# Two output rows assembled from a split last weight, in a recurrence followed by a soft mixture of experts on one Trainium2 core

## The chip, the core and the metric

The kernel runs on one core of a Trainium2 chip. The core has a matrix engine (TensorE, PE in the profile; its weight loads are PEld), a vector engine (VectorE, DVE), a scalar engine (ScalarE, ACT), a general engine (GpSimd, POOL) and a sync engine (SyncE, SP), which here issues the loads of the inputs and all stores. Weights are loaded from GpSimd's queue, which converts them to bf16 on the way. All transfers share 16 transfer engines. TensorE writes to PSUM, eight banks of 2 KB in each of 128 partitions, and the results are taken from there by VectorE or ScalarE.

The metric is the device time of one execution in microseconds, lower being better.

## The reference

Inputs are x and f_logit (4 batches, 5056 steps, 256 channels), a lower bound per channel, phi (256 x 32), w1 (8 experts, 256 x 1024) and w2 (8 experts, 1024 x 256). The output has 20224 rows of 256 channels, float32.

```python
def _attn_ref(x, f_logit, lower_bound):
    sig = 1.0 / (1.0 + np.exp(-f_logit))
    f = lower_bound + (1.0 - lower_bound) * sig
    i = 1.0 - f
    for t in range(S):
        h = f[:, t] * h + i[:, t] * x[:, t]
        y[:, t] = h

def _moe_ref(x, phi, w1, w2):
    logits = x @ phi                                # x: the rows of y, 20224 x 256
    d = softmax of logits over the rows             # one column per slot, 32 slots
    slot_input = d.T @ x                            # 8 experts x 4 slots, 256 channels
    for e in range(E):
        slot_out[e] = np.maximum(slot_input[e] @ w1[e], 0.0) @ w2[e]
    c = softmax of logits over the 32 slots
    return c @ slot_out
```

The two lines with "softmax of" stand for the written-out maximum, exponential and division. The slot inputs need every row of all batches, and every output row needs the slot outputs: no output can be finished before the last input has been read and the last weight applied.

## The kernel before, in words

**The first part** walks over units n of up to 512 steps of one batch: ten groups of four batches, 40 units. For each unit it loads f_logit and x, forms the sigmoid on ScalarE (L234), multiplies it with x on GpSimd (L245), turns both to channels by TensorE transposes (L249, L264), scans on VectorE (L332), turns the result back (L345, copied out at L364), and takes logits (L378) and their exponentials. The exponentials of all rows stay in `etall`, bf16, with 32 partitions for each batch: partition 32 b + s is slot s of batch b. Rows of 128 such columns are turned to tokens (L399) and multiplied with the scan's result into `slot_ps` (L428), which becomes the slot inputs. The order of all this is written by hand (`manual_schedule`, L157); the loop is at L499 to L595. Weights are loaded at units named in `W_AT`, by `load_w` on GpSimd's queue; the last weight, w2 of expert 7, comes in three pieces, of 4, 2 and 2 of its 8 chunks of 128 hidden channels (L144). In some units `idle` (L177) issues matmuls whose result isn't used, into the second half of the PSUM tile `slot_bank`, whose first half is `slot_ps`.

**The turn from the first part to the output** is at L596 to L710. `row_sums` (L407) sums the exponentials of the 32 slots for each row into `sums`, which lies in the PSUM tile `tail`; their reciprocals go to `rrow` and are the scales of the output rows. The slot inputs are taken from `slot_ps`, summed over the batches and turned to channels by four matmuls into `sin_ps` (L616 to L620), which is a part of `tail` too. They are scaled into `sin` (L631 on VectorE, L632 on ScalarE). The first layer (L648) makes `hi`, twice [128, 1024]: 32 partitions for each of four experts. The hidden values are turned by TensorE (L663) into `hid` (experts 0 to 3) and `wide` (experts 4 to 7, written out for all four batches). The second layer goes into one PSUM tile, `so_ps` (L696): 8 chunks of experts 4 to 7, and between them the sum over experts 0 to 3. `spin` (L707) then issues eight matmuls whose result isn't used. VectorE scales `so_ps` by `rcs`, the reciprocal of the sum of each slot's exponentials, into `slot_out` (L708), which has 32 partitions for each batch, and GpSimd makes from it `slot_bd` (L710), in which two batches stand side by side for one matmul.

**The output part** (from L713) has three kinds of stage, all made of one or several matmuls of `etall` with `slot_out` or `slot_bd`, an eviction with a scale by VectorE (`by_vector`, L717) or ScalarE (`by_scalar`, L721), and stores from SyncE's queue. `pieces` does the first 2048 rows of one batch, 16 rows for each partition, in five stores of growing size: 2, 2, 2, 4 and 6 rows for each partition. `by_rows` does the last block, two batches at a time (L760). `rest` does the last 64 rows of each batch. `whole` does the first 2048 rows of the other batches, one store each, and `couple` (L801) the second 2048 rows of two batches. The buffers come from pools: `osb` in SBUF, which takes the place of the first part's weights and loads, `pfirst` in PSUM, eight banks, and later `pout`. A pool that takes the place of released ones waits, at its first use, for the last use of everything in them.

Of the kernel before, what the change touches and what calls it, by code (L numbers as in the profile page):

```python
# [18 lines left out]
def kernel(  # L19
# [61 lines left out]

    nc.vector.tensor_copy(ident, ident_f)

    def rep_constants(b):
# [77 lines left out]
    with tc.tile_pool(name="sp2", bufs=3) as sp2, \  # L162
# [336 lines left out]
        for n in range(n_unit):  # L499
# [15 lines left out]
            else:  # L515
# [38 lines left out]
                if n in (n_unit - 5, n_unit - 4):  # L554
                    idle(2)
                elif n == SINGLE - 2:
                    idle(1, True)
                elif 2 * B <= n < n_unit - 4 and n % (2 * B) in (1, 5, 6, 7):
                    idle(1)
# [55 lines left out]
        nc.vector.tensor_copy(slot_sb, slot_ps)  # L615
        sin_ps = tail[:, 0, ds(G // 2, DC * NS)].rearrange("p (o s) -> p o s", o=DC)  # L616
        slot_v = slot_sb.rearrange("p (c o) -> p o c", o=DC)
# [6 lines left out]
    with tc.tile_pool(name="ew", bufs=1) as ew, \  # L624
# [16 lines left out]
        for q in range(E // Q):  # L641
            hi = ew.tile([P, F], BF16, name=f"hi{q}")
            for k in range(2):
# [10 lines left out]
                else:  # L654
                    nc.vector.tensor_scalar_max(hi[:, ds(k * H, H)], hi_ps, 0.0)
            his.append(hi)
        cs_ps = pm.tile([P, 1], F32, name="cs_ps", tag="pm")
        rcs = ew.tile([P, 1], F32, name="rcs")
        for q in range(E // Q):
# [4 lines left out]
            if q == 0:  # L664
                nc.tensor.matmul(cs_ps, rep2, cs1, start=True, stop=True)
                src = ht_ps.rearrange("p f (j s) -> p f j s", s=NS)[:, :, :, ds(0, SPE)]
                src = bass.AP(tensor=src.tensor, offset=src.offset,
                              ap=[list(src.ap[0]), [P, FC], [NS + SPE, Q], [1, SPE]])
                dst = hid[:, :, :, ds(0, SPE)]
                dst = bass.AP(tensor=dst.tensor, offset=dst.offset,  # L670
                              ap=[list(dst.ap[0]), [Q * NS, FC], [NS + SPE, Q], [1, SPE]])
                nc.scalar.copy(dst, src)
                nc.vector.reciprocal(rcs, cs_ps)
                continue
            for j in range(Q):
# [17 lines left out]
        nc.vector.reciprocal(rrow[:, :wide_r], rs_ps[:, :wide_r])  # L693
        for j in range(Q):
            for fc in range(FC):
                nc.tensor.matmul(so_ps, wide[:, fc, j].rearrange("p b s -> p (b s)"),  # L696
                                 w2_sb[Q + j][:, fc], start=j == 0 and fc == 0,
                                 stop=j == Q - 1 and fc == FC - 1, skip_group_check=True)
            if j == 0:
                nc.tensor.matmul(so_ps, rep2, so4, start=False, stop=False,  # L700
                                 skip_group_check=True)
                row_sums(2)
            if j == 1:
                q = n_grp * R - 1
                nc.vector.reciprocal(rrow[:, wide_r:q], rs_ps[:, wide_r:q])
                nc.vector.reciprocal(rrow[:, q, ds(0, B // 2)], rs_ps[:, q, ds(0, B // 2)])
        spin(tail[:, 1], 8, P)  # L707
        nc.vector.tensor_scalar_mul(slot_out, so_ps, rcs)  # L708
# [4 lines left out]
    held.close()  # L713
    with tc.tile_pool(name="osb", bufs=3) as osb:

# [21 lines left out]
        def pieces(i, b):  # L737
            dst = rows_of(i, b)
            ob = osb.tile([P, blocks[i][1], D], F32, name="ob", tag="ob")
            r0 = 0  # L740
            for k in (1, 1, 1, 2, 3):
                for j in range(2):
# [29 lines left out]
        end = len(blocks) - 1  # L772
        with tc.tile_pool(name="pfirst", bufs=8, space=PSUM) as pfirst:
            pieces(0, 0)
            by_rows(end, 0)
            by_rows(end, 1)
# [57 lines left out]
        rest()  # L834
        for b in range(1, B):
            whole(0, b)
# [33 lines left out]
```

## Time and profile before

| what | value |
|---|---|
| three runs | 196.96, 197.34, 197.62 us; median 197.34 |
| the profiled execution | 197.01 us |
| its span, first to last instruction | 195.2 us |
| mean granted TensorE clock | 0.845 of full speed |
| PE, PEld busy | 150.6 us (77%), 108.7 us (56%) |
| DVE, ACT, POOL busy | 142.0 us (73%), 138.8 us (71%), 103.1 us (53%) |
| HBM read and written | 58.23 MB, 20.71 MB |

A row of the timeline has the start in microseconds from the span's start, the time from the first start to the last end of the merged instructions, the engine, the line, and out<-in with shapes and count; in brackets stands the idle time before it and what ended it. A row of windows has the stretch, its length, the busy time of PE, PEld, DVE, ACT and POOL with the number of instructions, then the granted clock, the busy share of the 16 transfer engines and GB/s. For loads that convert float32 to bf16 the GB/s count the bytes written. A row of the chain of waits has start, length and what it was. In the lines of slices each digit is a tenth of the share, for one of 40 equal slices of the span. Matmuls overlap: their spacing, not the length of one, is the rate.

### The profile page before, as it was taken

Reading aid. Unit: us, or ns where it says so; the run is one execution under the profiler, and the core shown is the slowest. Engines: PE = TensorE matmul, PEld = TensorE weight load, DVE = VectorE, ACT = ScalarE, POOL = GpSimd, SP = SyncE. Lnnn points to the kernel's source line nnn. Section 1 sums busy time; section 2 is a strip of 40 time slices with the busy share of each in tenths; the row PEclk is TensorE's granted clock in tenths of the full one; section 3 lists DMA queues with packets and bytes.
Section 4 is the critical chain, followed back from the end, with each engine's and each line's share of the span. In section 5 each row is a group of like instructions: output and inputs, shape, how many; then the busy total and the mean of one; then the engine's idle time right before and its main releaser. Section 6 shows DMA issues by size and latency. Waiting matters only on the chain.

```text
span 195.2 us, 3283 instructions
## 1 busy us (share of the span) xinstructions
PE 150.6 (77%) x1222; PEld 108.7 (56%) x1222; DVE 142.0 (73%) x175; ACT 138.8 (71%) x192; POOL 103.1 (53%) x78
## 2 busy tenths in 40 slices
PE   0684896898998979989798976999997999980000
PEld 0474775765786657857576755766872663420000
DVE  2666699799699999999999999824288867770000
ACT  3686778599988998989988698724068788991000
POOL 2584888756798949776888979592030000000000
PEclk9998799699699999999999999999985555555555
DMA  6999999999999999999999999999949999999995
GB/s 203 415 433 428 426 425 421 430 426 411 326 428 426 423 334 405 423 425 414 324 418 418 235 212 214 214 212 211 170 165 428 425 431 426 430 433 430 430 430 218
DMA packets 12145, 70.75 MB, mean 362 GB/s; under 512 B 1361, under 2 KB 1874, under 8 KB 7650
## 3 DMA queue, kind: packets, MB, share of 16 engines
q1 hardware_dynamic: 9504, 62.13, 76.3%
q0 software_dynamic: 2624, 8.42, 21.8%
q8 instruction: 9, 0.15, 0.3%
q14 instruction: 6, 0.05, 0.1%
q10 hardware_dynamic: 2, 0.00, 0.0%
HBM read 58.23 MB, written 20.71 MB: 404 GB/s over the span
## 4 chain that ended last, share of the span: by engine, by line
PE 36%; DVE 28%; DMA 17%; ACT 4%; issue 4%; SPq 1%; POOL 0%; ACTq 0%
DVE h L332 17%; DMA w_t<-in_moe_w_dram 7%; PE op L801 7%; PE sp L249 7%; PE op L727 6%; DMA w_sb<-in_moe_w_dram 6%; PE hp L345 5%; DVE ht L364 5%; PE up L264 4%; DMA f_t<-in_f_logit_dram 4%; DVE h L319 3%; DVE oc L717 2%; PE op L760 2%; ACT s_t L234 1%; PE lg L378 1%
## 5 line engine op out<-in xcount | busy, mean ns | idle before, releaser
L245 POOL TENSOR_TENSOR u_t<-s_t,x_t 128x1024 bf16<-128x1024 bf16 (+1 forms) x39 | 82.4, 2129 | 24.5 <-ACT s_t L234 14.2
L332 DVE TENSOR_TENSOR_SCAN h<-a,h,up 128x512 bf16<-128x512 f32 x64 | 78.1, 1267 | 9.0 <-PE up L264 4.3
L234 ACT ACTIVATE s_t<-f_t 128x2048 bf16<-128x2048 f32 (+2 forms) x22 | 38.1, 1736 | 2.9 <-DMA f_t<-in_f_logit_dram 2.9
L345 PE MATMUL hp<-ident_f,h 128*128 128x128 f32 (+1 forms) x160 | 29.3, 307 | 8.4 <-DVE ht L364 6.3
L297 ACT ACTIVATE a<-sp,lbs 128x1024 f32<-128x1024 bf16 x28 | 29.6, 1112 | 4.6 <-PE sp L249 4.5
L345 PEld LDWEIGHTS hp<-ident_f,h 128*128 128x128 f32 (+1 forms) x160 | 23.2, 206 | 17.0 <-DVE ht L364 11.5
L249 PE MATMUL sp<-ident_f,s_t 128*128 128x128 f32 x144 | 23.7, 315 | 7.0 <-ACT s_t L234 5.7
L249 PEld LDWEIGHTS sp<-ident_f,s_t 128*128 128x128 f32 x144 | 19.6, 164 | 8.7 <-ACT s_t L234 6.5
L264 PE MATMUL up<-ident_f,u_t 64*128 64x64 f32 x224 | 21.4, 236 | 2.4 <-POOL u_t L245 2.4
L264 PEld LDWEIGHTS up<-ident_f,u_t 64*128 64x128 f32 x224 | 17.0, 144 | 7.1 <-POOL u_t L245 2.8
L721 ACT ACTIVATE ob<-op,rrow 128x256 f32<-128x256 f32 x32 | 12.4, 478 | 9.1 <-PE op L727 8.7
L364 ACT COPY ht<-hp 128x512 f32<-128x512 f32 (+1 forms) x21 | 12.2, 583 | 7.9 <-PE hp L345 7.9
L304 ACT ACTIVATE a<-sp,lbs 128x512 f32<-128x512 bf16 (+2 forms) x16 | 13.2, 868 | 2.9 <-PE sp L249 2.7
L183 PE MATMUL slot_ps<-rep,ident_f 128*128 128x256 f32 x42 | 14.2, 426 | 0.0
L364 DVE COPY ht<-hp 128x512 f32<-128x512 f32 (+1 forms) x19 | 12.7, 668 | 1.0 <-PE hp L345 1.0
L801 PE MATMUL op<-slot_bd,etall 64*128 64x512 bf16 x32 | 13.1, 627 | 0.0
L812 ACT ACTIVATE oc<-op,rrow 128x256 f32<-128x256 f32 x32 | 12.2, 486 | 0.8 <-PE op L801 0.3
L727 PE MATMUL op<-slot_out,etall 32*128 32x256 bf16 x64 | 12.6, 375 | 0.1
L806 DVE TENSOR_TENSOR oc<-op,rrow 128x1024 f32<-128x1024 f32 x8 | 9.7, 1223 | 3.4 <-PE op L801 3.4
L717 DVE TENSOR_TENSOR ob<-op,rrow 128x1024 f32<-128x1024 f32 (+2 forms) x12 | 9.8, 862 | 2.2 <-DMA out_dram<-ob 1.1
L727 PEld LDWEIGHTS <-etall 32*128 32x128 bf16 x64 | 8.9, 153 | 3.8 <-issue 1.3
L378 PE MATMUL lg<-h,phi 128*32 128x512 bf16 (+1 forms) x80 | 9.9, 389 | 0.2 <-ACT et L402 0.2
(109 smaller groups left out, 168.9 us busy)
## 6 DMA issues: line engine op xcount, KB each, us to landing
f_t<-in_f_logit_dram SPq DMA_DIRECT2D x14, 1024.0 KB, 11.2
x_t<-in_x_dram SPq DMA_DIRECT2D x14, 1024.0 KB, 9.5
out_dram<-oc SPq DMA_DIRECT2D x4, 2048.0 KB, 13.1
w_sb<-in_moe_w_dram POOLq DMA_DIRECT2D x14, 512.0 KB, 9.5
out_dram<-ob SPq DMA_DIRECT2D x3, 2048.0 KB, 9.6
f_t<-in_f_logit_dram SPq DMA_DIRECT2D x8, 512.0 KB, 7.0
x_t<-in_x_dram SPq DMA_DIRECT2D x8, 512.0 KB, 6.1
out_dram<-oc SPq DMA_DIRECT2D x4, 896.0 KB, 6.0
```

What stands on the lines that cost most here:

```text
L183: nc.tensor.matmul(slot_bank[:, 1], ident_f, wide_rep, start=False, stop=False, skip_group_check=True)
L234: nc.scalar.activation(s_t, f_t, ACT.Sigmoid, scale=-1.0)
L245: nc.gpsimd.tensor_tensor(uts[n][:, :r], s_t[:, :r], x_t[:, :r], ALU.mult)
L249: nc.tensor.transpose(ps[:, :, r], t[:, r].bitcast(F32), ident_f)
L264: nc.tensor.transpose(v[:, :, r], t(r)[k].bitcast(F32), ident_f[k, k])
L297: nc.scalar.activation(a, sp[:, :, :, :, o], ACT.Identity, scale=nomlb[:, ds(o, 1)], bias=1.0)
L332: nc.vector.tensor_tensor_scan(h[:, :T, o], decays[n // 2, o][:, n % 2, :T], up[:, :T, o], hs[number(g - 1, b)][:, ds(used(g - 1) - 1, 1), ...
L345: nc.tensor.transpose(hp[:n_p, r], hw[:, :n_p, r], ident_f)
L364: copy(hts[g][:n_p, b].rearrange("p r d -> p (r d)").bitcast(F32), hps.pop(n)[:n_p].rearrange("p r c -> p (r c)"))
L717: nc.vector.tensor_tensor(ob, op, scale.broadcast_to(list(ob.shape)), ALU.mult)
L727: nc.tensor.matmul(op[:, j], ew[:, :, r + j], slot_out[ds(b * NS, NS)], start=True, stop=True, skip_group_check=True)
L801: nc.tensor.matmul(op[:, i_r].rearrange("p u d -> p (u d)"), ew[:, :, r + i_r], slot_bd[ds(j * 2 * NS, 2 * NS)].rearrange("s u d -> s (u d)"),
```

## The change

The first store is taken from batch 3 and not batch 0, and its two rows for each partition are made in another way. `so_ps` is read by ScalarE when all but the last two chunks of expert 7 are in it; that part, for batch 3's 32 partitions, is scaled into `so_b`. What the last two chunks add is reordered: GpSimd multiplies the exponentials of those rows with `own` (which is `rcs` for the slots of expert 7 in batch 3 and zero elsewhere) into `near`; TensorE multiplies the hidden values of expert 7 with `near` into `near_ps`, and ScalarE copies that to `mix`. Each of the two rows is then three matmuls into one PSUM tile: exponentials with `so_b`, and `mix` with each of the two last weight chunks. They stand on TensorE behind the last two chunks' matmuls into `so_ps`, from which `slot_out` and `slot_bd` are made as before. `pieces` evicts these two rows first, in one store, and goes on with the rest.

Beside that, `sin_ps` moves from `tail` to the second half of `slot_bank`; the `idle` matmuls at unit 14 go; `spin` is no longer called; and `osb` and `pfirst` wait tile by tile (`reuse_waits="tile"`) and not for whole pools.

```diff
+    D3 = B - 1
+    own = consts.tile([P, 1], F32, name="own")
+    nc.vector.tensor_reduce(own, ident_f[:, ds(P - SPE, SPE)], AX.X, ALU.add)
...
-                elif 2 * B <= n < n_unit - 4 and n % (2 * B) in (1, 5, 6, 7):
+                elif 2 * B <= n < n_unit - 4 and n % (2 * B) in (1, 5, 6, 7) and n != 2 * B + 6:
                     idle(1)
...
-        sin_ps = tail[:, 0, ds(G // 2, DC * NS)].rearrange("p (o s) -> p o s", o=DC)
+        sin_ps = slot_bank[:, 1, ds(0, DC * NS)].rearrange("p (o s) -> p o s", o=DC)
...
+        LATE = FC // 4
+        k3 = ds(D3 * NS, NS)
+        near = ew.tile([P, 2, P], BF16, name="near")
...
                 nc.vector.reciprocal(rcs, cs_ps)
+                nc.vector.tensor_tensor(own, own, rcs, ALU.mult)
+                nc.gpsimd.tensor_scalar_mul(
+                    near[k3], etall[k3, ds(0, P * wide_r)].rearrange(
+                        "s (p r) -> s r p", r=wide_r)[:, ds(0, 2)], own[k3])
...
-        for j in range(Q):
-            for fc in range(FC):
-                nc.tensor.matmul(so_ps, wide[:, fc, j].rearrange("p b s -> p (b s)"),
-                                 w2_sb[Q + j][:, fc], start=j == 0 and fc == 0,
-                                 stop=j == Q - 1 and fc == FC - 1, skip_group_check=True)
-            if j == 0:
-                nc.tensor.matmul(so_ps, rep2, so4, start=False, stop=False,
-                                 skip_group_check=True)
-                row_sums(2)
-            if j == 1:
-                q = n_grp * R - 1
-                nc.vector.reciprocal(rrow[:, wide_r:q], rs_ps[:, wide_r:q])
-                nc.vector.reciprocal(rrow[:, q, ds(0, B // 2)], rs_ps[:, q, ds(0, B // 2)])
-        spin(tail[:, 1], 8, P)
+
+        def experts(dst, j, fcs, first=False, last=False):
+            for fc in fcs:
+                nc.tensor.matmul(dst, wide[:, fc, j].rearrange("p b s -> p (b s)"),
+                                 w2_sb[Q + j][:, fc], start=first and fc == fcs[0],
+                                 stop=last and fc == fcs[-1], skip_group_check=True)
+
+        experts(so_ps, 0, range(FC), first=True)
+        nc.tensor.matmul(so_ps, rep2, so4, start=False, stop=False, skip_group_check=True)
+        row_sums(2)
+        experts(so_ps, 1, range(FC))
+        q = n_grp * R - 1
+        nc.vector.reciprocal(rrow[:, wide_r:q], rs_ps[:, wide_r:q])
+        nc.vector.reciprocal(rrow[:, q, ds(0, B // 2)], rs_ps[:, q, ds(0, B // 2)])
+        near_ps = psu.tile([P, LATE, 2, P], F32, name="near_ps", tag="up")
+        hi_v = his[-1].rearrange("p (c f) -> p f c", f=FC)
+        for i in range(LATE):
+            nc.tensor.matmul(near_ps[:, i].rearrange("p r t -> p (r t)"),
+                             hi_v[k3, FC - LATE + i], near[k3].rearrange("s r t -> s (r t)"),
+                             start=True, stop=True, skip_group_check=True)
+        mix = ew.tile([P, LATE, 2, P], BF16, name="mix")
+        nc.scalar.copy(mix.rearrange("p f r t -> p (f r t)"),
+                       near_ps.rearrange("p f r t -> p (f r t)"))
+        experts(so_ps, 2, range(FC))
+        experts(so_ps, 3, range(FC - LATE))
+        so_b = ew.tile([P, D], BF16, name="so_b")
+        nc.scalar.activation(so_b[k3], so_ps[k3], ACT.Copy, scale=rcs[k3])
+        experts(so_ps, 3, range(FC - LATE, FC), last=True)
+        ops = []
+        for r in range(2):
+            op = pbig.tile([P, H], F32, name="hi_ps", tag=f"hi_ps{r}")[:, ds(0, D)]
+            ew_r = etall[k3, ds(0, P * wide_r)].rearrange("s (p r) -> s p r", r=wide_r)
+            nc.tensor.matmul(op, ew_r[:, :, r], so_b[k3], start=True, stop=False,
+                             skip_group_check=True)
+            for i in range(LATE):
+                nc.tensor.matmul(op, mix[:, i, r], w2_sb[E - 1][:, FC - LATE + i],
+                                 start=False, stop=i == LATE - 1, skip_group_check=True)
+            ops.append(op)
         nc.vector.tensor_scalar_mul(slot_out, so_ps, rcs)
...
-    with tc.tile_pool(name="osb", bufs=3) as osb:
+    with tc.tile_pool(name="osb", bufs=3, reuse_waits="tile") as osb:
...
         def pieces(i, b):
             dst = rows_of(i, b)
             ob = osb.tile([P, blocks[i][1], D], F32, name="ob", tag="ob")
-            r0 = 0
-            for k in (1, 1, 1, 2, 3):
+            for r in range(2):
+                (by_scalar, by_vector)[r](ob[:, ds(r, 1)], ops[r].unsqueeze(1),
+                                          scale_of(i, b, r, 1))
+            nc.sync.dma_start(out=dst[:, ds(0, 2)], in_=ob[:, ds(0, 2)])
+            r0 = 2
+            for k in (1, 1, 2, 3):
...
-        with tc.tile_pool(name="pfirst", bufs=8, space=PSUM) as pfirst:
-            pieces(0, 0)
+        with tc.tile_pool(name="pfirst", bufs=8, space=PSUM, reuse_waits="tile") as pfirst:
+            pieces(0, D3)
...
-        for b in range(1, B):
+        for b in range(D3):
             whole(0, b)
```

## The prediction

> **What bounds the kernel now.** I read the page's forty slices first (4.88 us each), then the chain of waits, then windows around the one slice where the transfers stop, then that slice's timeline.
>
> ```profile
> PEclk9998799699699999999999999999985555555555
> DMA  6999999999999999999999999999949999999995
> ```
>
> The transfer engines are full in every slice but the first, the last and the thirtieth (141.5 to 146.4 us). So the run is a load stream, a hole and a store stream; compute matters only where it makes the hole. The chain of waits through the hole:
>
> ```profile
> 126.92 14.59 DMA w_t<-in_moe_w_dram
> 141.56 0.39 PE so_ps L696 x2
> 141.98 0.49 DVE slot_out L708
> 142.52 1.96 PE op L727 x16
> ```
>
> The last piece of the last weight lands at 126.92 + 14.59 = 141.51; two matmuls, the scaling, the first output matmul and its eviction stand between it and the first store. The windows (last two columns: busy share of the transfer engines, GB/s) show how empty that is:
>
> ```profile
> 139.50:140.50 1.00, 1.00 (x12) 0.90 (x10) 0.07 (x2) 0.00 (x0) 0.00 (x0) 1.00 1.02 168
> 140.50:141.50 1.00, 0.79 (x7) 0.47 (x5) 0.00 (x0) 0.00 (x0) 0.00 (x0) 1.00 0.46 80
> 141.50:144.00 2.50, 2.31 (x24) 2.11 (x24) 1.60 (x5) 0.96 (x3) 1.36 (x2) 1.00 0.00 0
> 144.00:144.50 0.50, 0.48 (x5) 0.33 (x4) 0.50 (x2) 0.50 (x3) 0.47 (x1) 1.00 0.16 53
> 144.50:149.50 5.00, 4.74 (x14) 1.89 (x14) 4.84 (x10) 5.00 (x16) 0.00 (x0) 0.53 1.04 421
> 149.50:192.50 43.00, 24.26 (x82) 12.26 (x82) 19.26 (x18) 23.12 (x60) 0.00 (x0) 0.50 1.02 432
> ```
>
> From 144.5 on the engines never wait: 20.71 MB at about 430 GB/s is 48.2 us, whatever computes behind it. Share 0.16 in the half microsecond before 144.5 puts the first byte at about 144.42, some 0.84 after the first store is issued:
>
> ```profile
> 140.91 0.38 PE L696 MATMUL so_ps<-w_t,wide 128*128 128x256 bf16 x2
> 141.56 0.38 PE L696 MATMUL so_ps<-w_t,wide 128*128 128x256 bf16 x2 [0.27 <-DMA w_t<-in_moe_w_dram]
> 141.98 0.48 DVE L708 TENSOR_SCALAR slot_out<-so_ps,rcs 128x256 bf16<-128x256 f32 x1 [2.41 <-PE so_ps L696]
> 142.64 1.83 POOL L710 TENSOR_SCALAR slot_bd<-slot_out,parity 128x256 bf16<-128x256 bf16 x2 [9.69 <-DVE slot_out L708]
> 142.88 2.28 DVE L717 TENSOR_TENSOR ob<-op,rrow 128x256 f32<-128x256 f32 x5 [0.42 <-PE op L727]
> 143.04 1.93 ACT L721 ACTIVATE ob<-op,rrow 128x256 f32<-128x256 f32 x5 [6.96 <-PE op L727]
> 143.58 1.33 SPq L749 DMA_DIRECT2D out_dram<-ob  x3
> ```
>
> The number to move is 143.58 - 141.52 = 2.06 us. Whatever it loses, the end loses, as long as the stores behind keep the engines fed.
>
> **The slot inputs' own bank.** Today VectorE's read of sin_ps waits for row sums in other columns of the same tile:
>
> ```profile
> 129.85 0.61 PE L619 MATMUL tail<-rep,slot_sb 128*128 128x32 f32 x4
> 130.30 0.80 PE L411 MATMUL tail<-ones,etall 128*128 128x128 bf16 x10
> 131.21 0.25 DVE L631 TENSOR_SCALAR sin<-tail,lbs 128x32 bf16<-128x32 f32 x1 [1.49 <-PE tail L411]
> 131.52 2.07 PE L648 MATMUL hi_ps<-w_sb,sin 128*32 128x512 bf16 x32 [0.42 <-DVE sin L631]
> ```
>
> Its data are there at 129.85 + 0.61 = 130.46, so sin can start at 130.50 and everything to L696 moves up by up to 0.7 us. It buys nothing at the end: TensorE already catches up with the weights. The pieces of 256 and 128 KB before the last land at 123.55 + 16.7 = 140.25 and 124.44 + 16.4 = 140.85 (the page's issue rows; 16.4 because 15.5 is the median of it and 14.59), and the pair at 140.91 starts right behind the second. The 0.7 us becomes waiting for those landings. It does pay for what the change adds ahead of them: two near_ps matmuls of 32 rows by 256 (0.11 us each, the spacing in L727's row: (1.96 - 0.27) / 15). Without that cover they would cost 0.22.
>
> **Work hidden.** near on GpSimd: 0.92 us by L710's row, at about 134.9, where GpSimd has nothing until 142.64; needed near 139. The copy mix on ScalarE: 0.60 by the 128x512 eviction of L653, at about 139.5 to 140.1; ScalarE is idle from 136.1 to 143.04. own times rcs: under 0.2 on VectorE (L673's reciprocal took 0.17) in a gap of 0.80 before L679. own at the start: under 0.2, while VectorE waits for the first load until 9.52. Uncovered, each costs its duration.
>
> **so_b puts a wait ahead of the landing.** ScalarE reads rows 96 to 127 of so_ps after the pair of 140.91; the last two matmuls write that tile again, so TensorE must wait for the read. The pair ends at 140.91 + 0.38 = 141.29; 0.04 to start; the read is nearest to L721 (128x256 from PSUM, 0.47), between L632 (128x32, 0.29) and L653 (128x512, 0.60): I take 0.47; 0.05 back to TensorE: 141.85 (141.67 to 141.98). The landing alone would let it go at 141.56. So the change puts 0.29 on the path (0.11 to 0.42). Queued behind it on TensorE: the pair, the six new matmuls, every L727; on VectorE and GpSimd, slot_out and slot_bd.
>
> **From there to the store.** Eight matmuls: two into so_ps, three for each row. At 0.109 spacing (L696: eight in 1.03 us, (1.03 - 0.27) / 7) and 0.27 for the last, row 0 is ready at 141.85 + 4 x 0.109 + 0.27 = 142.56, row 1 at 142.88. slot_out runs 142.27 to 142.75 on VectorE, ahead of row 1's eviction, so that starts at 142.92 and takes 0.42; row 0 on ScalarE is done at 143.07. The issue today comes 0.07 after the later eviction: 143.34 + 0.07 = 143.41. Against 143.58: 0.17 earlier. Between 128-row and 32-row weights the spacing may be wider (L727's first two stand 0.17 apart, not 0.11), so 0.11 to 0.17; I take 0.13. The removed spin (0.61) ran beside slot_out and gives nothing.
>
> **Does the rest follow?** The second store needs row 2 on VectorE, 142.92 + 2 x 0.33 + 0.08 = 143.7, and row 3 on ScalarE, 143.75: issue at 143.82 against 144.03; a store of 256 KB lasts 0.61 us on the engines, so no gap. The thin place is by_rows: slot_bd ends 0.29 later (144.47 becomes 144.76), TensorE starts L760 at 144.81 and not 144.52, and VectorE's fourth eviction already waited there. If all 0.29 gets through, the store issued at 148.21 goes at 148.50, its bytes at 149.34; the first 2 MB would be drained at 144.29 + 2.10 MB / 425 GB/s = 149.2. Cost 0 to 0.15; I take 0, since the row gives only 0.16 of waiting.
>
> **Moved and renamed.** Taking batch 3 first changes addresses, not sizes: five stores of the same bytes on the same queue become one and four alike. Waits by tile drop wait instructions that had passed anyway: the store's last wait was for ScalarE's eviction. The idle matmuls at unit 14 (0.64 us of L183, at 58.08) are followed by a VectorE hole of 0.61 before L364 at 60.55; both go, but the engines for transfers are full there, so 0 at the end.
>
> **Sum:** -0.13 us (from -0.47 to +0.3). On the profiled execution, 195.2 span plus 1.8 around it = 197.01: 196.9. It was near the lowest of three (196.96); on the median 197.34 it is 197.2, which I forecast: no change, where 0.3% (0.59 us) is about what can be told from none.
>
> **Rivals.**
> *No hold.* If so_b's read doesn't stop the pair, TensorE goes at 141.56, the store at 143.12: 0.46 gained, 196.9. For: the read touches one quarter of the rows. Against: sin above waited for a whole tile. 0.15.
> *Slack counts.* The profiled execution had 0.1 us between compute and the landings; the median run is 0.33 slower. If that is compute arriving late, the 0.7 from sin removes it too: 197.34 - 0.33 - 0.13 to -0.46 = 196.9 to 196.5, faster by up to 0.4%. For: before 140.9 L696 runs without a wait, so compute, not landings, sets its pace there. Against: a full load stream cannot be late by compute. 0.25.
> *The clock falls first.* Slower. The granted clock was full until 144.8, half after:
>
> ```profile
> 141.40:144.82 3.42, 3.09 (x28) 2.67 (x28) 2.42 (x6) 1.78 (x5) 1.83 (x2) 1.00 0.11 43
> 144.82:148.23 3.41, 3.41 (x13) 1.54 (x12) 3.25 (x7) 3.41 (x11) 0.00 (x0) 0.50 1.06 425
> ```
>
> Today eight spin matmuls fill the gap to the first output. The change drops them and leaves TensorE idle from 141.29 to 141.85. If the drop comes before 141.85, the eight matmuls go at half speed: spacing 0.218 (48 of L727 in 10.67 us) adds 7 x 0.11, the longer last one 0.14, so the store goes at 144.3 and the time is 198.1, slower by 0.4%. It breaks even once the drop comes later than some 142.6. For: only the moment decides. Against: the stretch to 141.3 is as busy as before. 0.15; with the by_rows gap and a slow near, 0.2 for slower in all.
> The Trainium skill, "TensorE: Matmul & The Clock Gate", section "What's actually happening", says that the clock is judged over free-running windows of 3413 ns, not tied to the kernel's start. The drop at 144.82 and the half-speed stretches of 3.41 us agree; by it the moment shifts from one execution to the next, so this rival would show in some executions and not in others.
>
> **Chances.** Forecast 0.40, no hold 0.15, slack 0.25, clock and gap 0.20. Slack is over 0.3% in most of its span, and a no-hold run can pass it with the slack: faster 0.25. Slower 0.17. Same 0.58. Range 196.4 (slack and no hold) to 198.1 (clock); the forecast alone has 196.9 to 197.6.
>
> **What would show it.** The wait of the last w_t pair: on ScalarE's so_b (hold) or on the DMA. sin at about 130.5. The first store at 143.4, the first byte 0.84 later. The share of the transfer engines at 149 to 149.5. The clock between 141.4 and 143. It is wrong if the first store moves by more than 0.5 us, or if the engines pause after it.

## The result and the profile after

The changed kernel takes 199.61 us in the median of six runs (198.84 to 200.24), the kernel before 197.18 us beside it (196.94 to 197.62): slower, by a ratio of 1.0103 [1.0067, 1.0139]. The forecast was 197.2, its range ended at 198.1. Ratios and their intervals, here and below, leave out runs in a slower state, those more than 1.5% above the fastest of the same kernel, while medians and ranges hold every run, so that a kernel with the higher median can have the lower ratio. The profiled execution took 200.24 us, the slowest of the six, span 198.4 (before 197.01 and 195.2), mean clock 0.844 (0.845).

The line numbers have moved: the last weight's matmuls L696 are L708 now, `slot_out` L743, `slot_bd` L745, the evictions L752 (VectorE) and L756 (ScalarE), the other output rows' matmuls L762, `by_rows` L799, its store L809. New are `near` L682, `mix` L726, `so_b` L731, the row matmuls with `so_b` L737 and with `mix` L740. The first store is L778, the next four L788.

The slices of the page, 4.96 us each: the hole is still one place, somewhat deeper, and the clock still falls there.

```profile
PEclk9999979889997999999999999999985555555555
DMA  5999999999999999999999999999739999999996
```

The windows of the changed kernel, columns as before:

```profile
143.50:146.00 2.50, 1.83 (x10) 0.92 (x11) 0.99 (x3) 0.83 (x2) 0.95 (x2) 1.00 0.02 7
147.50:148.00 0.50, 0.50 (x4) 0.11 (x3) 0.50 (x2) 0.50 (x2) 0.00 (x0) 0.50 0.81 303
148.00:152.00 4.00, 4.00 (x15) 1.39 (x14) 3.23 (x6) 3.97 (x11) 0.00 (x0) 0.50 1.03 408
152.00:153.00 1.00, 0.43 (x2) 0.00 (x0) 1.00 (x3) 1.00 (x4) 0.00 (x0) 0.50 0.46 188
153.00:195.00 42.00, 24.27 (x82) 12.31 (x82) 19.50 (x19) 23.01 (x60) 0.00 (x0) 0.50 1.02 426
```

Two things are new. The transfer engines pause a second time, at 152 to 153 (share 0.46). And where they are full, they move 426 GB/s and not 432. The chain of waits and the timeline through the hole:

```profile
126.58 16.35 DMA w_t<-in_moe_w_dram
145.97 2.04 PE op L762 x13
148.01 3.17 PE op L799 x11
```

```profile
143.39 0.47 ACT L731 ACTIVATE so_b<-so_ps,rcs 32x256 bf16<-32x256 f32 x1 [1.87 <-PE so_ps L708]
143.91 0.38 PE L708 MATMUL so_ps<-w_t,wide 128*128 128x256 bf16 x2 [0.56 <-ACT so_b L731]
144.22 0.33 PE L737 MATMUL hi_ps<-so_b,etall 32*128 32x256 bf16 x1
144.40 0.48 DVE L743 TENSOR_SCALAR slot_out<-so_ps,rcs 128x256 bf16<-128x256 f32 x1 [3.96 <-PE so_ps L708]
144.48 0.39 PE L740 MATMUL hi_ps<-w_t,mix 128*128 128x256 bf16 x2
144.81 0.32 PE L737 MATMUL hi_ps<-so_b,etall 32*128 32x256 bf16 x1
145.06 0.39 PE L740 MATMUL hi_ps<-w_t,mix 128*128 128x256 bf16 x2
145.38 0.32 PE L762 MATMUL op<-slot_out,etall 32*128 32x256 bf16 x1
145.49 0.42 DVE L752 TENSOR_TENSOR ob<-hi_ps,rrow 128x256 f32<-128x256 f32 x1 [0.61 <-PE hi_ps L740]
145.97 2.04 PE L762 MATMUL op<-slot_out,etall 32*128 32x256 bf16 x13 [0.26 <-DVE ob L752]
145.98 0.35 SPq L778 DMA_DIRECT2D out_dram<-ob  x1
146.27 2.77 ACT L756 ACTIVATE ob<-op,rrow 128x256 f32<-128x256 f32 x7 [0.89 <-PE op L762]
146.77 2.62 SPq L788 DMA_DIRECT2D out_dram<-ob  x4
147.94 4.48 PE L799 MATMUL op<-slot_bd,etall 64*128 64x512 bf16 x14
151.93 0.81 SPq L809 DMA_DIRECT2D out_dram<-oc  x2
```

The chain no longer goes through the last piece of the last weight but through the piece before it, landed at 126.58 + 16.35 = 142.93: its pair of matmuls is what `so_b` reads, and the last pair waits for that reading (0.56). The last piece itself landed at 143.65 by the trace (before, 141.52). With the packets of the trace, the end can be split up:

| part, us | before | after | difference |
|---|---|---|---|
| last piece of the last weight lands | 141.52 | 143.65 | +2.13 |
| from there to the first byte of a store | 2.91 | 3.18 | +0.27 |
| time that the stores' packets take, over 16 engines | 49.03 | 49.67 | +0.64 |
| pauses of the engines among the stores | 0.09 | 0.39 | +0.30 |
| last byte | 193.55 | 196.89 | +3.34 |

The pauses are what is left between the first and the last byte when the packets' time is taken off. In *after_bank* below that comes out at -0.2 and is given as none, so it is good to some 0.2 us. Most of the loss lies where no instruction was moved: in the loads before the hole and in the stores behind it, whose bytes and number are the same (12145 packets, 70.75 MB in both). Single packets take longer:

| packets, median ns (mean) | before | after |
|---|---|---|
| loads of 8192 bytes, 3584 between 10 and 105 us | 309 (310.6) | 313 (314.5) |
| stores of 16384 bytes, between 155 and 190 us | 611 (611.5) | 615 (617.5) |
| stores of 7168 bytes, between 155 and 190 us | 272 (272.5) | 275.5 (277.9) |
| weights from GpSimd's queue, 4096 bytes read, between 10 and 105 us | 322 | 322 |

It is not the same surcharge on each packet. Before, the loads of 8192 bytes lie at 309 ns from the tenth to the ninetieth percentile; after, they spread from 309 to 320.

### The profile page after: what moved, and what is told of

Same layout as the page of the kernel before. It is cut to its first block, busy times and chain, and to the rows that moved or that the text cites. A ratio compares the mean times of both kernels' runs of the same rounds, so it can differ in the third digit from the quotient of the medians.

```text
span 198.4 us, 3284 instructions
## 1 busy us (share of the span) xinstructions
PE 151.8 (76%) x1218; PEld 107.8 (54%) x1218; DVE 142.8 (72%) x177; ACT 140.6 (71%) x194; POOL 104.3 (53%) x79
## 2 busy tenths in 40 slices
DMA packets 12145, 70.75 MB, mean 357 GB/s; under 512 B 1361, under 2 KB 1874, under 8 KB 7650
## 4 chain that ended last, share of the span: by engine, by line
PE 37%; DVE 20%; DMA 17%; ACT 8%; issue 4%; POOL 4%; SPq 1%; ACTq 0%; POOLq 0%
DVE h L336 12%; DMA w_t<-in_moe_w_dram 8%; PE op L840 7%; PE op L762 6%; PE sp L253 6%; PE hp L349 5%; DMA w_sb<-in_moe_w_dram 5%; PE up L268 5%; DMA f_t<-in_f_logit_dram 4%; ACT s_t L238 3%; POOL u_t L249 3%; DVE ht L368 3%; DVE h L323 3%; PE lg L382 2%; PE op L799 2%
## 5 line engine op out<-in xcount | busy, mean ns | idle before, releaser
L756 ACT ACTIVATE ob<-op,rrow 128x256 f32<-128x256 f32 x31 | 12.2, 475 | 3.0 <-PE op L762 2.6
L187 PE MATMUL slot_ps<-rep,ident_f 128*128 128x256 f32 x40 | 13.2, 421 | 1.3 <-DVE h L336 1.3
L762 PE MATMUL op<-slot_out,etall 32*128 32x256 bf16 x62 | 13.0, 390 | 0.3 <-DVE ob L752 0.3
L762 PEld LDWEIGHTS <-etall 32*128 32x128 bf16 x62 | 8.9, 155 | 4.1 <-issue 1.9
L752 DVE TENSOR_TENSOR ob<-op,rrow 128x1024 f32<-128x1024 f32 (+2 forms) x11 | 9.6, 904 | 1.9 <-PE op L762 1.7
L336 DVE TENSOR_TENSOR_SCAN h<-a,up 128x512 bf16<-128x512 f32 x8 | 9.3, 1206 | 2.0 <-PE up L268 1.1
```

The costliest lines, as they stand in the source:

```text
L187: nc.tensor.matmul(slot_bank[:, 1], ident_f, wide_rep, start=False, stop=False, skip_group_check=True)
L336: nc.vector.tensor_tensor_scan(h[:, :T, o], decays[n // 2, o][:, n % 2, :T], up[:, :T, o], hs[number(g - 1, b)][:, ds(used(g - 1) - 1, 1), ...
L762: nc.tensor.matmul(op[:, j], ew[:, :, r + j], slot_out[ds(b * NS, NS)], start=True, stop=True, skip_group_check=True)
```

## The experiments

Theory A: the line `own = consts.tile([P, 1], F32)` takes 32 bytes of each partition, ahead of the constant `ones`, of `etall` and of every tile behind them. In the build's address map `w1_sb0` starts at byte 32256 = 126 x 256 before and at 32288 after, and so do the load and store buffers behind it: 32 bytes past a multiple of 256. Theory B: the hole, by the hold of `so_b`, the spacing of the new matmuls, and the banks. Theory C: the clock, by the removed `idle` and `spin`.

### Addresses

`PAD` is unused columns behind `etall`; 16 of them are 32 bytes. *a_aligned* gives the 32 bytes back in the changed kernel (first diff); *b_shift32* puts the kernel before 32 bytes off (second diff), *b_shift64* and *b_shift128* 64 and 128 bytes, with 80 and 112.

```diff
-    PAD = 48
+    PAD = 32
```

```diff
-    PAD = 48
+    PAD = 64
```

> The changed kernel with 32 bytes less padding behind the exponentials, so that every tile that transfers write or read (inputs, weights, output buffers) begins at a multiple of 256 bytes again, as in the kernel before; in the changed kernel the new constant own moved them all by 32 bytes. Theory A (addresses): the packets of 8192 bytes go back from 313 ns to 309, the last weight lands near 141.5 to 142 us and not at 143.65, and the time falls by 1.3 to 2 us to 197.6 to 198.3 on the chip where the changed kernel takes 199.6; what is left over the kernel before (0.5 to 1 us) is the path behind the landing. Rival R (the removed idle matmuls or the other edits slow the loads): the landing stays at 143.6 and the time at 199 to 200.2.

> The kernel before with 32 bytes more padding behind the exponentials and nothing else: inputs, weights and output buffers begin 32 bytes behind a multiple of 256. Theory A: 1.3 to 2 us slower than the kernel before (198.5 to 199.2), packets of 8192 bytes at 313 ns. Rival R: no change, 197.2.

> The kernel before with those tiles 64 bytes behind a multiple of 256. Theory A, if only a start inside a 64-byte line costs: 197.2, no change. Theory A, if every start off 256 bytes costs: 198.5 to 199.2 as with 32 bytes. Rival R: no change.

> The kernel before with those tiles 128 bytes behind a multiple of 256. Theory A with a grain of 64 or 128 bytes: 197.2, no change. With a grain of 256 bytes: 198.5 to 199.2. Rival R: no change.

*b_shift32*: 198.77 us, ratio 1.0084 [1.0062, 1.0105]; *b_shift64*: 198.48, 1.0063 [1.0043, 1.0083]; *b_shift128*: 198.40, 1.0073 [1.0039, 1.0108]. The kernel before, with not one instruction changed, loses 1.2 to 1.7 us when its tiles start 32, 64 or 128 bytes past a multiple of 256. In *b_shift32* the last weight lands at 142.69 (+1.17), the stores' packets take 49.68 (+0.65), and the medians are those of the changed kernel (loads 313, stores 615). *a_aligned* has them back at 309 and 611, and the landing at 141.26; its profiled execution took 197.48, the fastest of its ten runs. But its timed runs went from 197.48 to 201.12, median 198.88, ratio 1.0076 [1.0038, 1.0115]: the address was not all.

*b_own* puts only `own` and its reduction into the kernel before and takes the 32 bytes from `PAD` (first diff). *a_nosh* puts `own` into unused bytes behind `lbs` in the changed kernel, as its last column (second diff), so that no transferred tile and no constant moves, not even `etall` and the small constants ahead of it, which in *a_aligned* are still 32 bytes off.

```diff
+    own = consts.tile([P, 1], F32, name="own")
+    nc.vector.tensor_reduce(own, ident_f[:, ds(P - SPE, SPE)], AX.X, ALU.add)
-    PAD = 48
+    PAD = 32
```

```diff
-    lbs = consts.tile([P, 2, DC], F32, name="lbs")
-    omlb, nomlb = lbs[:, 0], lbs[:, 1]
+    lbs = consts.tile([P, 2 * DC + 1], F32, name="lbs")
+    omlb, nomlb, own = lbs[:, ds(0, DC)], lbs[:, ds(DC, DC)], lbs[:, ds(2 * DC, 1)]
```

> The kernel before with the constant own and its one VectorE reduction at the start, unused after that, and 32 bytes less padding: ones, pair_ones, parity and the exponentials move by 32 bytes, inputs, weights and output buffers stay on multiples of 256. Theory P: the wide spread of the aligned changed kernel, median 198 to 199. Rival O: 197.0 to 197.3 with a narrow spread.

> The changed kernel with own put into the unused bytes behind lbs, so that no tile of the kernel before moves at all. The aligned version that had 32 bytes taken from the padding still moved ones, pair_ones, parity and the exponentials by 32 bytes, and its times spread from 197.5 to 201.1, by a load stream that in its slower executions is slower in places. Theory P (those places matter): the spread goes to that of the kernel before (nearly all within 0.5 us), median 197.3 to 197.6. Rival O (something else of the change, such as the longer program, makes the spread): median 198.5 to 199, spread 3 us as before.

*b_own*: 197.21, ratio 1.0000 [0.9973, 1.0027]. The reduction, the moved constants and the moved `etall` cost nothing; what costs is the address of the tiles behind `etall`, and the packets' times point to those that are transferred. The rows of GB/s in the two pages, of *b_own* and then of *b_shift32* (one number for each slice):

```profile
GB/s 202 419 431 427 428 430 420 428 423 424 319 426 427 421 325 416 425 423 403 334 418 419 243 207 214 215 212 215 161 166 428 423 435 430 426 430 430 430 430 218
```

```profile
GB/s 207 412 423 419 417 424 414 421 421 392 337 424 426 405 325 427 421 419 362 365 416 407 253 214 213 214 214 214 151 172 419 418 430 426 426 426 426 426 426 216
```

The reader is to compare the flat stretches: 430 against 426 at the end, 419 to 431 against 412 to 424 in the second to ninth slices. *a_nosh* gave 199.25 (197.62 to 202.16), 1.0053 [1.0018, 1.0089], so `etall` and the small constants are not what is left in *a_aligned*.

### Clock: the idle matmuls and the spin

Both on *a_aligned*: *a_al_idle* brings back the `idle` of unit 14 (first diff), *a_al_spin* puts eight spin matmuls ahead of the last pair into `so_ps` (second).

```diff
-                elif 2 * B <= n < n_unit - 4 and n % (2 * B) in (1, 5, 6, 7) and n != 2 * B + 6:
+                elif 2 * B <= n < n_unit - 4 and n % (2 * B) in (1, 5, 6, 7):
```

```diff
+        spin(tail[:, 1], 8, P)
         experts(so_ps, 3, range(FC - LATE, FC), last=True)
```

> The changed kernel with its tiles back on multiples of 256 bytes (197.5 to 201.1 us, median 198.9, against 197.0 for the kernel before), and with the idle matmuls of unit 14 put back. Theory C (clock): without them the TensorE clock falls in some executions near 60 us and the compute comes late to the weights, which makes the wide spread; then the median falls to 197.3 to 197.8 and the spread to under 1 us. Rival T (tail): the spread comes from behind the last landing; then the median stays at 198.5 to 199 and the spread at 3 us.

> The aligned changed kernel with the eight spin matmuls back, put between so_b's read and the last two chunks, where TensorE waits anyway. Theory T1 (the clock falls in the tail without them): the spread goes to under 1 us and the median to 197.3 to 197.8. Theory C, or any cause in front of the landing: no change, 198.5 to 199, spread 3 us.

*a_al_idle*: 199.09 (197.67 to 202.15), 1.0065 [1.0033, 1.0098]. *a_al_spin*: 199.06 (197.53 to 200.44), 1.0103 [1.0066, 1.0139]. Neither is better than *a_aligned*. The clock fell at 145.92 and 145.29, in *a_aligned* at 145.70: no later. Neither removed piece of idle work, put back alone, mends it.

### Banks and order

*a_al_bank* moves the two row tiles out of the banks of `hi_ps`, into the other bank of the pool that holds `near_ps` and into a bank of `tail`; the first two tiles of L762 then have banks that nobody reads any more.

```diff
-            op = pbig.tile([P, H], F32, name="hi_ps", tag=f"hi_ps{r}")[:, ds(0, D)]
+            op = (psu.tile([P, H], F32, name="op_r", tag="up") if r == 0 else tail[:, 1])[:, ds(0, D)]
```

> The aligned changed kernel with the two new rows' PSUM tiles in banks that the next output tiles use seventh and sixth, and not second and third. Theory B (bank): TensorE's matmul for row 3 no longer waits for VectorE's eviction of row 1 (0.26 us in the changed kernel's timeline), ScalarE's hole of 0.89 goes, the second store is issued 0.4 to 0.5 us behind the first and not 0.8, and the pause of the transfer engines between the first two stores (0.2 us) closes: 0.2 to 0.4 us. Rival: TensorE waits for slot_out anyway and the second store comes at the same 0.8.

It ran once: 197.42, span 195.7. That is 0.06 us under the fastest run of *a_aligned*, and from one time nothing follows; the order of events can be read. The lines of its timeline that answer to the last ones above:

```profile
143.37 1.74 PE L762 MATMUL op<-slot_out,etall 32*128 32x256 bf16 x14
143.84 2.67 ACT L756 ACTIVATE ob<-op,rrow 128x256 f32<-128x256 f32 x7 [0.47 <-PE op L762]
143.96 0.35 SPq L778 DMA_DIRECT2D out_dram<-ob  x1
144.41 2.45 SPq L788 DMA_DIRECT2D out_dram<-ob  x4
148.54 0.84 SPq L809 DMA_DIRECT2D out_dram<-oc  x2
```

L762 runs 14 matmuls without the wait on `ob` L752, ScalarE's wait is 0.47 and not 0.89, the second store comes 0.45 behind the first (0.79 in the changed kernel), the store of `by_rows` 4.58 behind (5.95), and the engines pause 0.10 us among the stores.

*a_fix* has that, the `idle` back, aligned tiles, and another order: the four matmuls with `mix` first, then the pair into `so_ps`, then the two with `so_b`, so that the hold by `so_b` covers them and the weights switch between 128 and 32 rows once. *fix_nosh* is the same with `own` behind `lbs`.

```diff
+        for r in range(2):
+            for i in range(LATE):
+                nc.tensor.matmul(ops[r], mix[:, i, r], w2_sb[E - 1][:, FC - LATE + i],
+                                 start=i == 0, stop=False, skip_group_check=True)
         experts(so_ps, 3, range(FC - LATE, FC), last=True)
...
+            nc.tensor.matmul(ops[r], ew_r[:, :, r], so_b[k3], start=False, stop=True,
+                             skip_group_check=True)
```

> The aligned changed kernel with the idle matmuls back, the new rows' tiles in late-used banks, and another order behind the landing: the four 128-row matmuls with mix first, then the last two chunks into so_ps, then the two 32-row matmuls with so_b. Theory: so_b's read is over by the time that so_ps is written (no hold), and there is one change between 128-row and 32-row weights and not four (0.21 to 0.26 us each in the changed kernel's timeline against 0.11): the first store 1.7 to 1.9 us behind the landing, against 2.06 in the kernel before and 2.33 to 2.41 in the changed one, and the time 196.6 to 197.0 against 197.0: same or up to 0.2% faster. Rival: slot_out, now 0.4 us later behind the landing than in the kernel before, makes the second and later stores late and the engines pause: 197.2 to 197.8.

> The version with the idle matmuls back, late-used banks and the mix matmuls first, with own in the unused bytes behind lbs, so that nothing is moved. From its timeline the first store comes 1.94 us behind the landing (2.06 in the kernel before) and the second 0.57 later. Theory P: 196.8 to 197.0 with a narrow spread, against 197.0 to 197.1 for the kernel before: same to 0.1% faster. Rival O: 197.7 with the spread of 3 us that it had.

*a_fix*: 197.69 (196.77 to 200.00), 1.0029 [1.0005, 1.0053]. *fix_nosh*: 197.49 (196.88 to 200.29), 0.9995 [0.9971, 1.0019]: as fast as the kernel before, not faster. From the timeline of *fix_nosh*, whose last weight landed at 141.69:

```profile
141.52 0.47 ACT L730 ACTIVATE so_b<-so_ps,rcs 32x256 bf16<-32x256 f32 x1 [2.36 <-PE so_ps L707]
141.82 0.38 PE L734 MATMUL op_r<-w_t,mix 128*128 128x256 bf16 x2 [0.34 <-DMA w_t<-in_moe_w_dram]
142.26 0.38 PE L707 MATMUL so_ps<-w_t,wide 128*128 128x256 bf16 x2
142.57 0.33 PE L739 MATMUL op_r<-so_b,etall 32*128 32x256 bf16 x1
143.63 0.35 SPq L776 DMA_DIRECT2D out_dram<-ob  x1
```

TensorE goes at the landing, the first store 1.94 behind it (2.33 in the changed kernel, 2.06 before). In this profile the idea gives 0.12 us at the first store; in *a_nosh_order* below it gives 0.22.

Three more runs took these repairs one by one. *a_nosh_bank* and *a_nosh_order* are *a_nosh* with the banks alone and with the order alone; *after_bank* is the changed kernel with the banks alone, its tiles still 32 bytes off.

> a_nosh with one thing more: the two row tiles lie in the banks of tail and near_ps, not in the banks of the first stages' tiles. If the wait for those banks is what puts the output matmuls into the stretch at half clock and makes the transfer engines pause, the pause goes from 1.50 us (a_nosh) to about 0.1, the second store is issued 0.45 us behind the first (0.79 before), the store of by_rows at most 4.8 us behind the first (6.62), and the runs gather at 197.3 to 197.8, median under 197.8, none but strays over 198.5. The rival, that the order of the eight matmuls behind the last weight does it: the median stays at 198.5 to 199.3 with runs from 197.5 to 201.

> a_nosh with the order of the eight matmuls alone changed: four with mix, the pair into so_ps, two with so_b; banks as in the change. The first row no longer waits for so_b's reading, so the first store is issued about 1.95 us behind the landing and not 2.41. The bank theory: the second store still comes 0.8 us behind the first, the pause stays at 0.5 us or more whenever the clock falls within 2 us of the first store, the median stays over 198.3. The order theory: median 197.3 to 197.8 and gathered.

> The changed kernel with the banks moved alone, own still ahead of the other constants, so every tile behind it starts 32 bytes off. Addresses alone are left to cost: 198.3 to 198.8 (the three shifted kernels before gave 198.40 to 198.77), gathered. If the two causes don't add up: 199.3 or more, or under 198.

| kernel | median (range), us | ratio | landing | landing to first store | pauses among stores |
|---|---|---|---|---|---|
| *a_nosh* | 199.25 (197.62–202.16) | 1.0053 [1.0018, 1.0089] | 143.74 | 2.34 | 1.50 |
| *a_nosh_bank* | 198.09 (197.33–200.05) | 1.0067 [1.0039, 1.0096] | 141.53 | 2.42 | 0.52 |
| *a_nosh_order* | 197.62 (196.97–199.78) | 1.0038 [1.0007, 1.0070] | 141.84 | 1.84 | 0.82 |
| *fix_nosh* | 197.49 (196.88–200.29) | 0.9995 [0.9971, 1.0019] | 141.69 | 1.94 | 0.36 |
| *after_bank* | 198.97 (198.84–200.58) | 1.0101 [1.0072, 1.0130] | 142.98 | 2.41 | none |

None of the three came out as expected in full. The order gives its half microsecond, and the second store still comes 0.79 behind the first, as the bank theory said; but the median is 197.62, where the order theory had it, though the runs are not gathered. The banks bring the second store to 0.45, but the store of `by_rows` still comes 5.65 behind the first, the pause is 0.52 and not 0.1, and by the intervals the banks alone are not shown to gain. *after_bank* lies 0.2 us above the highest of the shifted kernels before and its ratio is that of the changed kernel (1.0101, 1.0103): here too the banks alone gain nothing that the times show.

The pauses go with the moment at which the clock falls. The windows of *a_nosh*, where it fell 0.24 us after the first store was issued (146.08), and of *after_bank*, where it fell 2.98 after (145.39):

```profile
146.00:147.00 1.00, 0.93 (x6) 0.80 (x6) 0.77 (x3) 0.63 (x2) 0.97 (x2) 0.66 0.05 20
149.00:150.00 1.00, 1.00 (x3) 0.30 (x2) 0.61 (x1) 1.00 (x4) 0.00 (x0) 0.50 0.84 344
152.00:153.00 1.00, 1.00 (x3) 0.15 (x1) 1.00 (x2) 1.00 (x4) 0.00 (x0) 0.50 0.51 209
```

```profile
147.00:148.00 1.00, 1.00 (x7) 0.49 (x6) 1.00 (x3) 1.00 (x4) 0.00 (x0) 1.00 1.01 379
149.00:150.00 1.00, 1.00 (x4) 0.35 (x3) 1.00 (x3) 1.00 (x5) 0.00 (x0) 0.50 1.07 430
```

TensorE is busy nearly all through both, at half clock from 146.3 in the one and from 148.4 in the other; only the first lets the transfer engines run dry. The two differ in banks and addresses as well, so here are all the profiles, by when the clock fell after the first store's issue:

| kernel | clock falls, us after | store of `by_rows`, us after | pause, us |
|---|---|---|---|
| *a_nosh* | 0.24 | 6.62 | 1.50 |
| *a_nosh_bank* (banks) | 0.41 | 5.65 | 0.52 |
| *after_again* | 0.53 | 6.34 | 0.81 |
| changed kernel | 0.95 | 5.95 | 0.39 |
| *a_nosh_order* (order) | 0.96 | 5.95 | 0.82 |
| *a_al_idle* | 0.96 | 5.94 | 0.81 |
| *a_al_spin* | 1.12 | 5.78 | 0.66 |
| *a_aligned* | 2.0 | 5.05 | 0.58 |
| *after_bank* (banks) | 3.0 | 4.58 | none |
| *a_al_bank* (banks) | 3.0 | 4.58 | 0.10 |
| *a_fix* (banks, order) | 6.7 | 4.70 | 0.12 |
| *fix_nosh* (banks, order) | 7.2 | 4.70 | 0.36 |
| kernel before | 1.24 | 4.63 | 0.09 |
| kernel before with *b_own* or shifted, four kernels | 2.6 to 3.6 | 4.37 to 4.38 | 0.07 to 0.20 |

At the same moment of the clock the kernel before issues this store more than a microsecond earlier than the changed one. With the same banks and the same order of matmuls, *a_al_bank* and *a_nosh_bank*, a fall at 3.0 and at 0.41 goes with 4.58 and 5.65 us for this store. These are single executions, and the pause doesn't follow the moment alone: with the fall at 0.95 and 0.96 it is 0.39 and 0.82, and *fix_nosh*, where it fell latest, has 0.36. That a delayed store at half clock makes the pause is read from these profiles; no run sets the moment of the clock.

*after_again*, the changed kernel once more, expected as

> The changed kernel itself, on the same chip as the three others, for the difference between them: 198.8 to 200.2 us by all theories; the version with own behind lbs below it by 1.2 to 2 us by the theory of addresses (4 ns on each packet of 8192 bytes, 1.8 us in all when the kernel before is moved by 32 bytes).

gave 199.96 (198.91 to 201.54), 1.0127 [1.0064, 1.0190]; its last weight landed at 142.76 and its store packets took 49.64, so of the 2.13 us by which the landing of the first profile was late, 1.24 is in both profiles and the rest was the first one's own.

On the changed kernel itself two pairs differ in the place of `own` alone: *after_again* and *a_nosh* (medians 199.96 and 199.25), *after_bank* and *a_nosh_bank* (198.97 and 198.09). The address is worth 0.7 and 0.9 us there, by intervals that overlap; only on the kernel before do the times alone show it.

## Why the prediction was wrong

**The step that failed first** is the one that cost `own` at nothing: "own at the start: under 0.2, while VectorE waits for the first load until 9.52", and the one sentence on addresses, "Taking batch 3 first changes addresses, not sizes", is about those of the stored rows. The instruction does cost nothing (*b_own*). I looked at what it does and not at where its four bytes lie: they push the weights, the load buffers and the store buffers off their 256-byte starts, which costs 1.2 to 1.7 us by the three shifted kernels before. The prediction had no term and no rival for it, and it is more than the whole distance from the forecast to the range's end. The terms fit: 3584 loads, 3.9 ns more each in the mean, over 16 engines are 0.87 of the 1.17 us by which *b_shift32* lands later; its last 1024 loads of 4096 bytes, 2.8 ns more each (159.8 to 162.6), are another 0.18; the stores add 0.65. Both signs that the prediction named for being wrong came: the first store at 145.98 and not 143.4 (2.13 of that is the landing), and a pause after it.

The Trainium skill, "DMA: Bandwidth & Descriptors", section "How a descriptor splits into AXI transactions", says that a transaction must start at a multiple of 256 bytes and that a descriptor which doesn't start there begins with the part from the boundary below, its unused bytes paid for. The traces agree in kind: packets to and from the shifted tiles take longer. By the Trainium skill's count there of 32-byte beats, a start 32 bytes off adds one beat to the 256 of 8192 bytes and one 128 bytes off adds four; the estimate from that, 1.2 and 4.8 ns of 309, doesn't fit: the mean load packet takes 3.9 ns more at 32 bytes, 3.0 at 64 and 2.5 at 128. A price for one more transaction in each packet doesn't fit either, since the packets spread from 309 to 320 and the converting loads of the weights, whose tiles moved as well, stay at 322. How a shifted start comes to cost this is open.

**sin: right, and for the reason given.** VectorE's wait for it is 0.87 and on the slot inputs' own matmuls, not on row sums, and nothing of it shows at the end, though no run has this edit alone:

```profile
132.03 0.25 DVE L635 TENSOR_SCALAR sin<-slot_ps,lbs 128x32 bf16<-128x32 f32 x1 [0.87 <-PE slot_ps L623]
```

**Work hidden: right.** `near` took 1.21 us (0.92 predicted), `mix` 0.59 (0.60). `near` was done at 137.1, 3.4 us before the `near_ps` matmuls began.

**The hold of so_b: right.** The pair waits on ACT L731, `so_b` takes the predicted 0.47, and the pair starts at 143.91, 0.26 after its weight landed (141.85 - 141.51 = 0.34 predicted). The rival without a hold falls.

**From there to the store: the spacing was mis-sized.** From the pair's start to the end of the last row matmul I had 0.109 between matmuls, 1.03 us; it is 143.91 to 145.06 + 0.39 = 145.45, 1.54 us. L708 to L737 to L740 and back stand 0.20 to 0.26 apart at each change between weights of 128 and of 32 rows, four changes. I allowed 0.04 us for them, read from one pair of L727 that has no such change. So the first store came 2.33 behind the landing and not 1.9; in *fix_nosh*, with one change, 1.94.

**Does the rest follow: half right.** I named the thin place, `by_rows`, but let only the 0.29 of the hold reach it and then took 0. What reached it was more. Row 3 was to follow at once, with the second store 0.41 behind the first; it came 0.79 behind. Row 3's tile lies in the bank of row 1's and waits for VectorE's eviction (0.26 on TensorE, 0.89 on ScalarE); 13 of the 14 matmuls of L762 begin when the first store goes, where L727 began 1.06 us before it; so the first of L799 starts 1.96 behind the first store (before, as the lines below show, 144.52 - 143.58 = 0.94; predicted 144.81 - 143.41 = 1.40). ScalarE can't make up its 0.89: it is busy for 3.97 of the 4.00 us from 148 to 152. The store of `by_rows` comes 5.95 behind the first and not 4.63, and at half clock that delay goes with a pause.

```profile
144.52 4.74 PE L760 MATMUL op<-slot_bd,etall 64*128 64x512 bf16 x14
148.21 4.02 SPq L770 DMA_DIRECT2D out_dram<-oc  x4
```

**The rivals.** *Slack counts* has no support: with addresses, banks and order mended, the time is that of the kernel before (0.9995), though the interval's end at 0.9971 doesn't rule out its smaller gains. *The clock falls first* had the right piece in the wrong place. In no profile did it fall ahead of the eight matmuls, but its moment, which differs between executions, decides how much of the output matmuls runs at full speed, and the changed kernel left less reserve there than the one before. The free-running windows of the Trainium skill, "TensorE: Matmul & The Clock Gate", section "What's actually happening", cited in the prediction, fit this: the fall came between 144.36 and 153.28 us in the profiles.

**What stays open.** The mended kernels' shares can't be told apart by the times: the intervals of *a_nosh*, *a_nosh_bank* and *a_nosh_order* overlap, and only those of *a_nosh_bank* and *fix_nosh* are apart. In *a_nosh* the last weight also landed 2.2 us later than in *a_nosh_bank*, with the same edits ahead of it; why single executions load more slowly no run shows. Whether the moment of the clock explains the whole spread of the changed kernels (197.6 to 202.2 in *a_nosh*) isn't shown either; the pauses that go with it are 1.5 us at most.

## What to carry to other kernels

In a kernel that a load and a store stream bound, a new small tile is costed by what it does to the addresses of all tiles behind it: take its bytes from padding, or put it last, and compare the mean time of a packet before and after; the median can hide it (loads of *b_shift128*: median 309 as before, mean 313.1 against 310.6). A shortcut on the critical path is worth only what it saves after its own switches of weight shape, and it spends the time in which the work behind it used to get ahead; look at how late the second and sixth store may be, not only the first. And reuse of PSUM banks has to be checked for the tile after the next.

## What was not expected of the hardware

- A start 32, 64 or 128 bytes past a multiple of 256 costs 3.9, 3.0 and 2.5 ns in the mean for each packet of 8192 bytes loaded (310.6 before), and some 4 ns in the median for each of 16384 bytes stored (611 to 615): 0.6 to 0.8% of this kernel. Converting loads of 4096 bytes from GpSimd's queue don't change (322).
- A change between matmul weights of 128 and of 32 rows takes 0.20 to 0.26 us from start to start where like follows like in 0.11. The weights of 32 rows here are columns of `etall` 16 apart, those of 128 rows lie close; no run separates the rows from the stride.
